# Layernorm of the next block moved between the gate and up steps of a gated MLP, with program order kept on three engines

## The chip, the cores and the metric

One core of one Trainium2 chip. The metric is the device time of one execution in microseconds, on the slowest (here the only) core. Profiled spans run from the first to the last instruction and are about 2 us shorter than the times.

## The reference, cut to what matters

```
xn = layernorm(x)                                  # x: 2048 x 640, bf16
s  = attention(xn)                                 # 32 heads of 192, last 512 keys, then @ wo
g  = silu((sigmoid(xn @ w_gate) * (xn @ w_up)) @ w_down)   # 640 -> 1536 -> 640
out = x + s * g
```

The kernel does the layernorm and the MLP first, in four blocks of 512 rows (g goes out to memory, the transposed xn stays on chip), then attention. The change touches the first part only.

## The kernel before: the parts concerned

One tile is 128 rows; a block has four. `xnT` is the transposed, normalised x that both parts read.

```python
def emit_ln_tile(i, xt, lnsb, lnps):
    xn = lnsb.tile([P, D], BF16, tag="xn")
    if i % 3 != 2:
        ...                                        # bn_stats x2, bn_aggr on DVE
    else:
        nc.scalar.activation(out=junk[:], in_=xt, func=ACT.Identity, accum_out=s12[:, 0:1])
        nc.scalar.activation(out=junk[:], in_=xt, func=ACT.Square, accum_out=s12[:, 1:2])
        ...                                        # three small DVE operations
    nc.scalar.activation(out=std[:], in_=var_ap, func=ACT.Sqrt, bias=eps_t[:], scale=1.0)
    nc.vector.reciprocal(out=rstd[:], in_=std[:])
    nc.vector.tensor_scalar(out=xn[:], in0=xt, ...)          # (x - mean) * rstd
    tps = lnps.tile([P, ND, P], BF16, tag="tps")             # one PSUM buffer
    for kt in range(ND):
        nc.tensor.transpose(tps[:, kt, :], xn[:, kt * P:(kt + 1) * P], ident[:])
    if i % 2 == 0:
        nc.scalar.copy(out=xnT[:, :, i * P:(i + 1) * P], in_=tps[:])
    else:
        nc.vector.tensor_copy(out=xnT[:, :, i * P:(i + 1) * P], in_=tps[:])
...
load_x(0)                                          # two buffers for x
...                                                # w_gate, w_up, w_down, one DMA each
load_x(1)
for tcn in range(NTC):                             # four blocks
    for tt in range(TPC):
        emit_ln_tile(tcn * TPC + tt, xt_c[:, tt, :], lnsb, lnps)
    if tcn + 2 < NTC:
        load_x(tcn + 2)
    for ft in range(NF):                           # twelve steps
        ...                                        # gps: 5 matmuls, ups: 5 matmuls
        nc.scalar.activation(out=sig[:], in_=gps[:], func=ACT.Sigmoid)
        nc.vector.tensor_tensor(out=hT[:, ft, :], in0=ups[:], in1=sig[:], op=ALU.mult)
    for tt in range(TPC):
        ...                                        # yps: w_down matmuls, silu, store g
```

The order on each engine is not that of the text: a scheduler sorts the instructions at compile time (in the trace of this kernel statistics of block 2 stand on ACT ahead of block 0's first copy, which starts at 26.02).

The softmax here doesn't subtract the row's maximum and nothing guards it: scores larger than these inputs give would overflow.

## Time and profile before

Median 1077.68 us of 4 runs. The prediction below shows the lines; this table puts the points in time together. "First" and "last" are starts of the first and ends of the last matmul, from the trace's order in time.

| us | before |
|---|---|
| first gate matmul of block 0 | 30.90 |
| 12 gate and up steps, blocks 0 to 3 | 27.83, 28.55, 27.75, 27.43 |
| gap from last w_down matmul to next first gate matmul | 4.57, 4.32, 4.32 |
| end of the MLP (last w_down matmul) | 207.6 |
| attention, from there to the end | 867.9 |

The step times run to the end of the last matmul; in a stream without gaps the next one starts about 0.16 us before that. In the gaps and the first 31 us PE has only the transposes to do. Attention is PE-bound (97% busy) and not touched.

### The profile page before, as it was taken

How to read it: one execution, taken by the hardware profiler on the slowest of the kernel's cores; microseconds unless marked ns; L12 is line 12 of the kernel's file. 1: busy time of each engine (PE TensorE's matmuls, PEld its weight loads, DVE VectorE, ACT ScalarE, POOL GpSimd, SP SyncE). 2: the span in 40 equal slices, each digit the busy share in tenths (PEclk: the TensorE clock that was granted, in tenths of full speed). 3: DMA queues.
4: the chain of work that ended last, by engine and by line, in shares of the span. 5: the costliest groups of instructions: out<-in, count | busy, mean ns of one | idle time of the engine just before them, and what ended most of it. 6: DMA issues, size and time to landing. Idle time of an engine off the chain costs nothing.

```text
span 1075.5 us, 18642 instructions
## 1 busy us (share of the span) xinstructions
PE 1014.6 (94%) x7362; PEld 579.6 (54%) x7472; DVE 426.8 (40%) x1545; ACT 439.7 (41%) x840; POOL 207.4 (19%) x337
## 2 busy tenths in 40 slices
PE   0989898999999999999999999999999999999998
PEld 0444444456565655555555555655555555555654
DVE  3433332245555520445445105445441055445502
ACT  3732222354545430265565203565561045565400
POOL 3000000233333210222222003222220032222000
PEclk9989999999999999999999999999999999999999
DMA  9200000284444334633233247233323563233042
GB/s 337 77 25 1 25 13 12 70 269 119 116 122 113 97 95 150 208 97 95 85 86 100 83 147 232 75 99 100 85 82 101 162 206 97 81 89 100 16 129 68
DMA packets 52039, 114.59 MB, mean 107 GB/s; under 512 B 5104, under 2 KB 34800, under 8 KB 51952
## 3 DMA queue, kind: packets, MB, share of 16 engines
q0 software_dynamic: 21424, 75.38, 23.9%
q1 hardware_dynamic: 30528, 38.01, 11.1%
q8 instruction: 58, 0.95, 0.4%
q14 instruction: 29, 0.24, 0.1%
HBM read 108.13 MB, written 5.24 MB: 105 GB/s over the span
## 4 chain that ended last, share of the span: by engine, by line
PE 77%; ACT 13%; issue 4%; DMA 4%; DVE 1%; POOL 0%; ACTq 0%; POOLq 0%
PE qps L254 20%; PE s_ps L326 19%; PE ops L291 16%; ACT pT L280 6%; ACT pT L279 5%; PE gps L174 5%; PE yps L193 5%; PE ups L179 5%; PE scB L273 2%; PE scA L270 2%; DMA xt<-in_A_x_dram 2%; PE scA L276 2%; DMA v_sb<-in_A_v_cache_dram 2%; PE kps L248 1%; ACT xnT L136 0%
## 5 line engine op out<-in xcount | busy, mean ns | idle before, releaser
L279 ACT ACTIVATE pT<-scA 128x512 bf16<-128x512 f32 x256 | 159.5, 623 | 209.4 <-PE scB L277 209.4
L254 PE MATMUL qps<-xnT,wq_sb 128*128 128x512 bf16 x901 | 214.3, 379 | 10.5 <-ACT pT L279 7.3
L326 PE MATMUL s_ps<-wo_sb,oT 128*128 128x128 bf16 (+1 forms) x1504 | 208.3, 297 | 2.5 <-ACT pT L279 0.5
L258 ACT CAST qT<-qps 128x512 bf16<-128x512 f32 x192 | 114.1, 594 | 231.7 <-PE qps L254 231.7
L297 DVE TENSOR_SCALAR o_sb<-ops,rden 128x192 bf16<-128x192 f32 x512 | 192.3, 407 | 4.5
L291 PE MATMUL ops<-v_sb,pT 128*128 128x193 bf16 x2048 | 181.5, 247 | 0.5 <-ACT pT L279 0.4
L291 PEld LDWEIGHTS <-pT 128*128 128x128 bf16 x2048 | 172.4, 98 | 15.9 <-ACT pT L279 1.0
L326 PEld LDWEIGHTS <-oT 128*128 128x128 bf16 x1536 | 118.1, 98 | 91.3 <-issue 2.0
L296 DVE RECIPROCAL rden<-ops 128x1 f32<-128x1 f32 x512 | 83.2, 163 | 204.2 <-PE ops L291 198.5
L280 ACT ACTIVATE pT<-scB 128x512 bf16<-128x512 f32 x256 | 161.7, 632 | 0.0
L254 PEld LDWEIGHTS <-wq_sb 128*128 128x128 bf16 x960 | 92.7, 97 | 111.5 <-issue 12.8
L310 DVE COPY oT<-otp 128x384 bf16<-128x384 bf16 x256 | 73.8, 349 | 102.6 <-PE otp L309 102.6
L228 POOL DMA_DIRECT2D wq_sb<-in_A_wq_dram x64 | 54.7, 854 | 278.3 <-PE qps L254 253.3
L233 POOL DMA_DIRECT2D v_sb<-in_A_v_cache_dram x128 | 96.3, 756 | 33.9 <-issue 23.8
L338 DVE TENSOR_TENSOR sg<-s_ps,gt 128x512 f32<-128x512 f32 (+1 forms) x32 | 14.2, 485 | 186.3 <-PE s_ps L326 183.1
L276 PE MATMUL scA<-qT,kTc 64*128 64x512 bf16 x256 | 77.1, 381 | 0.0
L277 PE MATMUL scB<-qT,kTc 64*128 64x512 bf16 x256 | 77.1, 381 | 0.0
L270 PE MATMUL scA<-qT,kTc 128*128 128x512 bf16 x255 | 76.6, 382 | 0.0
L273 PE MATMUL scB<-qT,kTc 128*128 128x512 bf16 x256 | 76.2, 379 | 0.1
L174 PE MATMUL gps<-xnT,wg_sb 128*128 128x512 bf16 x234 | 63.7, 400 | 3.2 <-DVE xnT L138 2.3
L185 DVE TENSOR_TENSOR hT<-ups,sig 128x512 bf16<-128x512 f32 x48 | 33.0, 691 | 77.7 <-PE ups L179 70.4
L179 PE MATMUL ups<-xnT,wu_sb 128*128 128x512 bf16 x235 | 61.3, 390 | 0.2
(54 smaller groups left out, 555.4 us busy)
## 6 DMA issues: line engine op xcount, KB each, us to landing
wq_sb<-in_A_wq_dram POOLq DMA_DIRECT2D x64, 480.0 KB, 4.2
wo_sb<-in_A_wo_dram SPq DMA_DIRECT2D x24, 1280.0 KB, 6.4
v_sb<-in_A_v_cache_dram POOLq DMA_DIRECT2D x128, 192.0 KB, 3.2
k_sb<-in_A_k_cache_dram POOLq DMA_DIRECT2D x32, 192.0 KB, 3.3
xt<-in_A_x_dram SPq DMA_DIRECT2D x4, 640.0 KB, 5.4
xt<-in_A_x_dram POOLq DMA_DIRECT2D x16, 160.0 KB, 3.5
gt<-g_dr POOLq DMA_DIRECT2D x16, 160.0 KB, 3.2
out_dram<-ot SPq DMA_DIRECT2D x16, 160.0 KB, 3.1
```

Of the source, the lines that this page charges most:

```text
L174: nc.tensor.matmul(gps[:], lhsT=wg_sb[:, kt, ft * P:(ft + 1) * P], rhs=xnT[:, kt, t0:t0 + TC], start=(kt == 0), stop=(kt == ND - 1),)
L179: nc.tensor.matmul(ups[:], lhsT=wu_sb[:, kt, ft * P:(ft + 1) * P], rhs=xnT[:, kt, t0:t0 + TC], start=(kt == 0), stop=(kt == ND - 1),)
L254: nc.tensor.matmul(qps[:, 0:TC], lhsT=wq_sb[:, kt, jj * P:(jj + 1) * P], rhs=xnT[:, kt, t0:t0 + TC], start=(kt == 0), stop=(kt == ND - 1),)
L258: nc.scalar.copy(out=qT[:, jj, :], in_=qps[:, 0:TC])
L270: nc.tensor.matmul(scA[st][:, 0:TC], lhsT=kTc[:, pr, 0, ss], rhs=qT[:, 0, :], start=True, stop=False)
L273: nc.tensor.matmul(scB[st][:, 0:TC], lhsT=kTc[:, pr, 2, ss], rhs=qT[:, 2, :], start=True, stop=False)
L276: nc.tensor.matmul(scA[st][:, 0:TC], lhsT=kTc[0:64, pr, 1, ss], rhs=qT[0:64, 1, :], start=False, stop=True)
L279: nc.scalar.activation(out=pTs[0][:, st, :], in_=scA[st][:, 0:TC], func=ACT.Exp, scale=SCALE)
L280: nc.scalar.activation(out=pTs[1][:, st, :], in_=scB[st][:, 0:TC], func=ACT.Exp, scale=SCALE)
L291: nc.tensor.matmul(ops[:, 0:DH + 1], lhsT=pT[:, st, ti * P:(ti + 1) * P], rhs=v_sb[:, st, hx, 0:DH + 1], start=(st == 0), stop=(st == NS - 1),
L297: nc.vector.tensor_scalar(out=o_sb[:, ti, hx * DH:(hx + 1) * DH], in0=ops[:, 0:DH], scalar1=rden[:, 0:1], scalar2=None, op0=ALU.mult,)
L326: nc.tensor.matmul(s_tiles[ti][ci][:, 0:cw], lhsT=oT[:, jt, ti * P:(ti + 1) * P], rhs=wo_sb[:, jl, cc0:cc0 + cw], start=(jt == 0), stop=(j ...
```

## The change

Its intent is to keep PE busy through the MLP: block 0's layernorm by a hand-written order, every later block's layernorm spread over the steps of the block ahead of it, and a fixed order so that the scheduler cannot undo it. With it come four x buffers in place of two, the gate and up weights in thirds, a dummy Sqrt at the beginning, and statistics of all later tiles on DVE.

```diff
-        tc.tile_pool(name="ln_x", bufs=2) as lnx,
+        tc.tile_pool(name="ln_x", bufs=4) as lnx,
+        tc.manual_schedule(engines={ENG.PE, ENG.Activation, ENG.DVE}),
...
-        nc.gpsimd.dma_start(out=wg_sb[:], in_=B_w_gate.rearrange("(kt p) f -> p kt f", p=P))
-        nc.gpsimd.dma_start(out=wu_sb[:], in_=B_w_up.rearrange("(kt p) f -> p kt f", p=P))
+        FCH = 3
+        for fc in range(FCH):
+            fs = slice(fc * F // FCH, (fc + 1) * F // FCH)
+            nc.gpsimd.dma_start(out=wg_sb[:, :, fs], in_=wg_v[:, :, fs])
+            nc.gpsimd.dma_start(out=wu_sb[:, :, fs], in_=wu_v[:, :, fs])
...
+        warm = lnsb.tile([P, 1], F32, tag="warm")
+        ln_std(warm[:], eps_t[:])                 # the dummy Sqrt
...                                                # block 0's layernorm, in a fixed order
+                if xt_n is not None:              # after step ft: the next block
+                    if ft < TPC:
+                        ...
+                        ln_stats(mv_n[:, ft, :], xt_n[:, ft, :], lnsb)
+                        if ft == TPC - 1:
+                            ln_std(std_n[:], mv_n[:, :, 1])
+                            nc.vector.reciprocal(out=rstd_n[:], in_=std_n[:])
+                    elif ft % 2 == 0:
+                        if ft > 4:
+                            tt = (ft - 6) // 2
+                            ln_tr((tcn + 1) * TPC + tt, xn_n, lnps, tt % 2 == 0)
+                        tt = (ft - 4) // 2
+                        xn_n = ln_norm(xt_n[:, tt, :], mv_n[:, tt, 0:1], rstd_n[:, tt:tt + 1], lnsb)
+                    elif ft == NF - 1:
+                        ln_tr((tcn + 1) * TPC + TPC - 1, xn_n, lnps, False)
```

`ln_stats`, `ln_std`, `ln_norm` and `ln_tr` are the parts of the old `emit_ln_tile`; `ln_tr` is the five transposes and the copy.

More of the change, by code (lines that the diff above doesn't have):

```diff
@@ L97 @@
     fsz = D // nchunk
-    def emit_ln_tile(i, xt, lnsb, lnps):
-        xn = lnsb.tile([P, D], BF16, tag="xn")
-        if i % 3 != 2:
-            stats = lnsb.tile([P, nchunk, nc.vector.BN_STATS_DIM], F32, tag="stats")
-            for c in range(nchunk):
-                nc.vector.bn_stats(out=stats[:, c, :], in_=xt[:, c * fsz:(c + 1) * fsz])
-            mv = lnsb.tile([P, nc.vector.BN_AGGR_DIM], F32, tag="mv")
-            nc.vector.bn_aggr(out=mv[:], in_=stats[:])
-            mean_ap = mv[:, 0:1]
-            var_ap = mv[:, 1:2]
-        else:
-            junk = lnsb.tile([P, D], BF16, tag="junk")
-            s12 = lnsb.tile([P, 2], F32, tag="s12")
-            nc.scalar.activation(out=junk[:], in_=xt, func=ACT.Identity, accum_out=s12[:, 0:1])
-            nc.scalar.activation(out=junk[:], in_=xt, func=ACT.Square, accum_out=s12[:, 1:2])
-            mvs = lnsb.tile([P, 2], F32, tag="mvs")
-            nc.vector.tensor_scalar(out=mvs[:, 0:1], in0=s12[:, 0:1], scalar1=1.0 / D, scalar2=None, op0=ALU.mult)
-            m2 = lnsb.tile([P, 1], F32, tag="m2")
-            nc.vector.tensor_tensor(out=m2[:], in0=mvs[:, 0:1], in1=mvs[:, 0:1], op=ALU.mult)
-            nc.vector.scalar_tensor_tensor(
-                out=mvs[:, 1:2], in0=s12[:, 1:2], scalar=1.0 / D, in1=m2[:],
-                op0=ALU.mult, op1=ALU.subtract,
-            )
-            mean_ap = mvs[:, 0:1]
-            var_ap = mvs[:, 1:2]
-        std = lnsb.tile([P, 1], F32, tag="std")
-        nc.scalar.activation(out=std[:], in_=var_ap, func=ACT.Sqrt, bias=eps_t[:], scale=1.0)
-        rstd = lnsb.tile([P, 1], F32, tag="rstd")
-        nc.vector.reciprocal(out=rstd[:], in_=std[:])
@@ new lines, in ln_stats, with ln_std, ln_norm @@
+    def ln_stats(mv_ap, xt, lnsb):
+        stats = lnsb.tile([P, nchunk, nc.vector.BN_STATS_DIM], F32, tag="stats")
+        for c in range(nchunk):
+            nc.vector.bn_stats(out=stats[:, c, :], in_=xt[:, c * fsz:(c + 1) * fsz])
+        nc.vector.bn_aggr(out=mv_ap, in_=stats[:])
+    def ln_std(std_ap, var_ap):
+        nc.scalar.activation(out=std_ap, in_=var_ap, func=ACT.Sqrt, bias=eps_t[:], scale=1.0)
+    def ln_norm(xt, mean_ap, rstd_ap, lnsb):
+        xn = lnsb.tile([P, D], BF16, tag="xn")
@@ L128, in emit_ln_tile, with ln_tr @@
         nc.vector.tensor_scalar(
-            out=xn[:], in0=xt, scalar1=mean_ap, scalar2=rstd[:],
-            op0=ALU.subtract, op1=ALU.mult,
-        )
+            out=xn[:], in0=xt, scalar1=mean_ap, scalar2=rstd_ap, op0=ALU.subtract, op1=ALU.mult,
+        )
+        return xn
+    def ln_tr(i, xn, lnps, on_act):
         tps = lnps.tile([P, ND, P], BF16, tag="tps")
@@ L134, in emit_ln_tile @@
             nc.tensor.transpose(tps[:, kt, :], xn[:, kt * P:(kt + 1) * P], ident[:])
-        if i % 2 == 0:
+        if on_act:
             nc.scalar.copy(out=xnT[:, :, i * P:(i + 1) * P], in_=tps[:])
@@ L138, in emit_ln_tile @@
             nc.vector.tensor_copy(out=xnT[:, :, i * P:(i + 1) * P], in_=tps[:])
+    ENG = mybir.EngineType
     with (
-        tc.tile_pool(name="ln_x", bufs=2) as lnx,
+        tc.tile_pool(name="ln_x", bufs=4) as lnx,
         tc.tile_pool(name="ln_sb", bufs=4) as lnsb,
@@ L147 @@
         tc.tile_pool(name="mlp_ps1", bufs=1, space=bass.MemoryType.PSUM) as mps1,
+        tc.manual_schedule(engines={ENG.PE, ENG.Activation, ENG.DVE}),
     ):
         xtiles = {}
-        def load_x(tcn):
+        for tcn in range(NTC):
             xt = lnx.tile([P, TPC, D], BF16, tag="xt")
@@ L154, in load_x @@
             xtiles[tcn] = xt
-        load_x(0)
-        nc.gpsimd.dma_start(out=wg_sb[:], in_=B_w_gate.rearrange("(kt p) f -> p kt f", p=P))
-        nc.gpsimd.dma_start(out=wu_sb[:], in_=B_w_up.rearrange("(kt p) f -> p kt f", p=P))
-        nc.gpsimd.dma_start(out=wd_sb[:], in_=B_w_down.rearrange("(kt p) d -> p kt d", p=P))
-        if NTC > 1:
-            load_x(1)
+        wg_v = B_w_gate.rearrange("(kt p) f -> p kt f", p=P)
+        wu_v = B_w_up.rearrange("(kt p) f -> p kt f", p=P)
+        FCH = 3
@@ new lines @@
+        for fc in range(FCH):
+            fs = slice(fc * F // FCH, (fc + 1) * F // FCH)
+            nc.gpsimd.dma_start(out=wg_sb[:, :, fs], in_=wg_v[:, :, fs])
+            nc.gpsimd.dma_start(out=wu_sb[:, :, fs], in_=wu_v[:, :, fs])
+        nc.gpsimd.dma_start(out=wd_sb[:], in_=B_w_down.rearrange("(kt p) d -> p kt d", p=P))
+        warm = lnsb.tile([P, 1], F32, tag="warm")
+        ln_std(warm[:], eps_t[:])
+        x0 = xtiles[0]
+        mv0 = [lnsb.tile([P, 2], F32, tag="mv", name=f"mv{t}") for t in range(4)]
@@ new lines, with norm0 @@
+        std0 = [lnsb.tile([P, 1], F32, tag="std", name=f"std{t}") for t in range(4)]
+        rstd0 = [lnsb.tile([P, 1], F32, tag="rstd", name=f"rstd{t}") for t in range(4)]
+        junk = lnsb.tile([P, D], BF16, tag="junk")
+        s12 = lnsb.tile([P, 2], F32, tag="s12")
+        m2 = lnsb.tile([P, 1], F32, tag="m2")
+        def norm0(t):
+            nc.vector.reciprocal(out=rstd0[t][:], in_=std0[t][:])
+            return ln_norm(x0[:, t, :], mv0[t][:, 0:1], rstd0[t][:], lnsb)
+        nc.scalar.activation(out=junk[:], in_=x0[:, 2, :], func=ACT.Identity, accum_out=s12[:, 0:1])
@@ new lines @@
+        ln_stats(mv0[0][:], x0[:, 0, :], lnsb)
+        ln_std(std0[0][:], mv0[0][:, 1:2])
+        nc.scalar.activation(out=junk[:], in_=x0[:, 2, :], func=ACT.Square, accum_out=s12[:, 1:2])
+        ln_stats(mv0[1][:], x0[:, 1, :], lnsb)
+        ln_std(std0[1][:], mv0[1][:, 1:2])
+        n0 = norm0(0)
+        n1 = norm0(1)
+        ln_tr(0, n0, lnps, True)
+        nc.vector.tensor_scalar(out=mv0[2][:, 0:1], in0=s12[:, 0:1], scalar1=1.0 / D, scalar2=None, op0=ALU.mult)
+        nc.vector.tensor_tensor(out=m2[:], in0=mv0[2][:, 0:1], in1=mv0[2][:, 0:1], op=ALU.mult)
@@ L162 @@
+        nc.vector.scalar_tensor_tensor(
+            out=mv0[2][:, 1:2], in0=s12[:, 1:2], scalar=1.0 / D, in1=m2[:], op0=ALU.mult, op1=ALU.subtract,
+        )
+        ln_stats(mv0[3][:], x0[:, 3, :], lnsb)
+        ln_std(std0[2][:], mv0[2][:, 1:2])
+        ln_std(std0[3][:], mv0[3][:, 1:2])
+        ln_tr(1, n1, lnps, True)
+        n2 = norm0(2)
+        ln_tr(2, n2, lnps, True)
+        n3 = norm0(3)
+        ln_tr(3, n3, lnps, False)
         for tcn in range(NTC):
             t0 = tcn * TC
-            xt_c = xtiles.pop(tcn)
@@ L165 @@
-            for tt in range(TPC):
-                emit_ln_tile(tcn * TPC + tt, xt_c[:, tt, :], lnsb, lnps)
-            if tcn + 2 < NTC:
-                load_x(tcn + 2)
+            xt_n = xtiles.get(tcn + 1)
+            xn_n = None
             hT = mh.tile([P, NF, TC], BF16, tag="hT")
@@ L185 @@
                 nc.vector.tensor_tensor(out=hT[:, ft, :], in0=ups[:], in1=sig[:], op=ALU.mult)
+                if xt_n is not None:
+                    if ft < TPC:
+                        if ft == 0:
+                            mv_n = lnsb.tile([P, TPC, 2], F32, tag="mvn")
+                            std_n = lnsb.tile([P, TPC], F32, tag="stdn")
+                            rstd_n = lnsb.tile([P, TPC], F32, tag="rstdn")
+                        ln_stats(mv_n[:, ft, :], xt_n[:, ft, :], lnsb)
[10 more added lines that the diff above has]
+                        ln_tr((tcn + 1) * TPC + TPC - 1, xn_n, lnps, False)
             for tt in range(TPC):
```

## The prediction

Its sum is: 16.9 + 13.2 + 6.0 - 3.4 - 0.5 = 32.2 us, and 1077.7 - 32.2 = 1045.5.

> **What bounds the kernel now.** I read the page first: which engine is full, and where it is not.
>
> ```profile
> PE 1014.6 (94%) x7362; PEld 579.6 (54%) x7472; DVE 426.8 (40%) x1545; ACT 439.7 (41%) x840; POOL 207.4 (19%) x337
> PE   0989898999999999999999999999999999999998
> ```
>
> PE is nearly full, so time can be won only where it is not: the first slice (27 us) and slices 3, 5 and 7, all in the first 208 us, the MLP stage that the diff edits. Next, the busy time by stretch, cut at the first matmul of each of the four 512-row blocks and at the last one before it (columns: PE, PEld, DVE, ACT, POOL busy, granted clock, DMA share, GB/s).
>
> ```profile
> 0.00:30.90 30.90, 2.79 (x20) 2.14 (x21) 12.86 (x57) 13.14 (x33) 11.43 (x21) 1.00 0.96 330
> 71.40:76.10 4.70, 2.00 (x23) 1.48 (x21) 3.52 (x12) 3.06 (x5) 0.55 (x1) 0.82 0.09 35
> 117.50:122.00 4.50, 1.81 (x24) 1.33 (x22) 3.04 (x8) 1.84 (x4) 0.54 (x1) 1.00 0.10 36
> 162.70:167.10 4.40, 1.72 (x23) 1.24 (x21) 1.87 (x4) 1.75 (x4) 0.54 (x1) 0.94 0.10 37
> 207.70:1075.50 867.80, 844.69 (x6436) 495.41 (x6527) 357.74 (x1378) 366.58 (x706) 192.17 (x309) 1.00 0.39 116
> ```
>
> So there are four holes: 31 us before block 0 and about 4.5 us before each of the other three. Attention (last row) takes 868 us at full clock with PE at 97%; the diff has no line there. The chain of waits says what fills the first hole:
>
> ```profile
> 0.74 4.42 DMA xt<-in_A_x_dram
> 5.19 1.28 DVE stats L104 x3
> ...
> 11.89 13.38 DMA xt<-in_A_x_dram
> 25.29 0.83 ACT junk L112 x2
> 26.12 0.58 ACT xnT L136
> ```
>
> The x of block 0 lands at 5.16, but 13.4 us go to another load of x, begun at 11.89. That is the third block's (two buffers, so it waits for block 0's x to be used up). Block 0 does not need it. The order on ACT makes it wait: the waits of PE give the price.
>
> ```profile
> PE tps L134 <- ACT xnT L136: 23.0, 8, 17.4
> PE tps L134 <- DVE xn L128: 8.6, 1, 8.6
> PE gps L174 <- DVE xnT L138: 2.3, 4, 0.6
> ```
>
> The longest wait, 17.4 us, is for an ACT copy of transposed x. The timeline shows tile 0 transposed at 8.62 to 9.34 and copied only at 26.02: ACT was given statistics of block 2 ahead of it, and stood still until that x came. The remaining 5.6 us of the row are copies between transposes, one PSUM buffer for all, at the three later boundaries and in block 0.
>
> [...] the ready copy sat 16.7 us behind a waiting instruction. [...] at 30.90, 76.12, 122.03 and 167.14 the first matmuls start 0.43 us apart, then 0.216, and the clock records say 0.5 for 6.8, 3.4 and 3.4 us around the three later boundaries. [...] The trace has 11 loads in this stage, 1283 ns each[...] (37.75 to 40.65 us holds two loads and the Sqrts: 2.9 us). [...] while block 2's x and w_down ran together (16 to 23 us), they shared, x getting 20% of the time; but at the start x of blocks 0 and 1 (1.3 MB) ran alone to 5.6 us, though w_gate was issued at 1.29.
>
> **The change, part by part.**
>
> *Start.* PE, ACT and DVE now keep program order, so block 2's statistics cannot overtake block 0's copies. I lay the new chain out with durations of the old trace. x lands at 5.16 as before (first in its queue). A dummy Sqrt loads the table during the load of x; so the 1.28 us load at 6.03 is out of the way (Identity and Square ran after the Sqrt load without another). Tile 0: two bn_stats (0.43 start to start) and aggregate (0.2) to 6.4; Sqrt 0.29, to 6.75, while DVE does tile 1's statistics to 7.45; reciprocal 0.15 and normalise 0.44, to 8.05. First transpose about 8.1 (before: 8.62). Then the single PSUM buffer sets the pace: cold transposes 0.70, copy 0.67 on ACT or 0.49 on DVE, two semaphores of 0.04 to 0.1, so 1.47 per tile on ACT, 1.27 on DVE (measured 28.02 minus 26.75). Tile 1 starts at 9.6; its copy stands in ACT's order behind tile 3's Sqrt, whose statistics DVE ends at about 10.2; so it ends at 11.2. Tiles 2 and 3: 11.3 and 12.75; first gate matmul 12.75 + 1.27 = **14.0**. Gain 30.9 - 14.0 = **16.9 us**.
>
> Are the weights there? They now come in thirds, 0.655 MB each. With four x buffers all four loads of x queue at once, so blocks 2 and 3 compete with them. If these share as at 16 to 23 us (0.29 MB/us for weights, from 5.8): gate third at about 8.6, up third at 10.9. If x runs first as at the start: its 2.62 MB at 0.37 MB/us end near 9.7, gate third 12, up third 14, needed at 16. Either way before PE, and each next third has 4 x 2.16 = 8.6 us of matmuls before it. This needs waits by region of a tile, which the trace shows: at 149.83 w_down matmuls read hT while its last slice was still being written (149.89 to 150.58).
>
> *Boundaries.* Statistics, normalising and transposes of the next block move between the 12 steps of this block's gate and up matmuls. Removed: gaps from last yps to first gps, 71.55 to 76.12, 117.71 to 122.03, 162.82 to 167.14: 4.57 + 4.32 + 4.32 = **13.2 us**. With the gap goes the half clock. A warm step is 2.158 us (11 steps from 170.83 to 194.57), so 12 are 25.9; blocks 1 to 3 took 28.55, 27.75 and 27.43 from first gps to first yps: 2.65 + 1.85 + 1.53 = **6.0 us**. Added on PE: 12 sets of five transposes in the stream at 0.055 each (12 kps transposes fill 0.66 us), 12 x 0.28 = **3.4 us**.
>
> *Room on the others.* Per step of 2.16 us DVE has hT 0.69, and in steps 0 to 3 two bn_stats and an aggregate, 1.1: 1.8 in all, it fits. ACT has 0.60 and sometimes a 0.69 copy. The tight place is step 3: Sqrt waits for all statistics, 1.9 us after the up matmuls of step 3, then Sqrt 0.29 and a Sigmoid load 1.28 (the Sqrt load fits in the wait). Sigmoid 4 then ends 4.15 us after that point and frees the bank for gate step 6, which starts at 4.3. Just hidden; I allow 0.17 us in each of three blocks, **0.5 us**.
>
> Sum: 16.9 + 13.2 + 6.0 - 3.4 - 0.5 = **32.2 us**. Cross-check: 14.0 + 4 x (25.9 + 13.04) + 1.8 cold at the start + 3.4 + 0.5 = 175.5 for the end of the MLP against 207.6. Time: 1077.7 - 32.2 = **1045.5 us**.
>
> **Rivals.** (a) Weights take over the wait: if a matmul waits for whole weight tiles, or small pieces run slower, PE starts near 20, when both (3.93 MB at 0.29 from 5.8) are in; about 1051. For: DMA share is 0.96 in the first 31 us. Against: the region waits above, and pieces of 5 x 1024 bytes per partition are near w_down's 5120-byte packets, which kept 354 GB/s (my working: 16 engines, 231 ns each). (b) Fixed order stalls PE inside the blocks: the table switch, or a transpose waiting for its input. One lost step per block, 3 x 2.2, makes 1052. For: margins of 0.2 us at step 3. Against: block 0 of before had two table loads and four passes over x on ACT from 36.16 to 40.65, and PE lost only 0.17 us. (c) The MLP gains but attention gives some back: another order of its instructions, or its prefetches (now behind three times as many weight loads on POOL) late. For: POOL already waits 4.1 us for w_gate to land before a ninth load. Against: there are over 150 us until the first is used. Worth perhaps plus or minus 4 us. (d) Only the start gains and the boundaries stay serial: 1061; it would need the copies or normalisations to slip past the block, against 2.16 us steps with over half of ACT free.
>
> **Range and chances.** The start is good to 1.5 us, the clock recovery to 1 us, stalls inside blocks 0 to 5 us, attention 2 us: low 1040, high 1052. The 2% line is 1056.1; it would take (a) and (b) together or (d). Chances: faster 0.93, same 0.06, slower 0.01.
>
> **What would show it.** First gate matmul at 14 (19 or later: rival a, with a DMA of w_gate or w_up ahead of PE). First yps about 27.7 us later, then blocks repeating every 40 us instead of 45 to 46, with no half clock after about 18. No PE wait for an xnT copy after block 0. Waits of gps or ups for sig or hT around the fifth to seventh steps would be (b). MLP end at 175.5 and attention 868 long; a different length there is (c). I am wrong on mechanism if blocks still take 45 us.

## The result, and the profile after

1045.34 us (median of 8, 1044.31 to 1045.78) against 1077.77 (12 runs): a ratio of 0.9701, 95% interval 0.9691 to 0.9711. Ratios in this document are the mean time of one kernel's fast runs over that of the other's in the same rounds, so not quite the ratio of the medians quoted. Predicted: 1045.5.

The page's PE rows, busy share and busy tenths by slice:

```profile
PE 1007.9 (97%) x7362; PEld 578.2 (55%) x7472; DVE 430.4 (41%) x1535; ACT 429.0 (41%) x814; POOL 211.7 (20%) x341
PE   5999999999999999999999999999999999999998
```

The zero of the first slice is a 5 and the 8s are gone. PE's busy time fell by only 6.7 us while the span fell by 32: most of the gain is idle time, the rest matmuls no longer at half clock.

Busy time by stretch, cut at the first gate matmul of each block (columns as in the prediction):

```profile
0.00:14.20 14.20, 2.79 (x20) 2.14 (x21) 6.83 (x22) 7.43 (x14) 9.62 (x17) 1.00 0.89 298
56.40:96.50 40.10, 39.84 (x235) 20.29 (x238) 18.15 (x39) 14.85 (x26) 1.10 (x2) 1.00 0.05 17
...
175.60:1043.50 867.90, 844.70 (x6437) 495.62 (x6527) 358.20 (x1378) 366.75 (x706) 190.59 (x305) 1.00 0.39 116
```

A block now takes 40.0 us in place of 45 to 46 and PE is busy in all of it, with DVE at 18 us of 40. Attention takes 867.9 us, to the tenth what it took.

The chain of waits over the start:

```profile
0.74 4.37 DMA xt<-in_A_x_dram
...
10.83 0.59 ACT xnT L120
...
11.46 0.70 PE tps L118 x5
12.19 0.70 ACT xnT L120
...
12.94 0.71 PE tps L118 x5
13.67 0.50 DVE xnT L122
...
14.21 2.29 PE gps L194 x5
```

No DMA stands in it but the first x. From 5.1 to 10.5 us (left out above) nearly every piece is DVE, with statistics and normalises; from 10.8 us on it is the pattern of one PSUM buffer: copy, transpose, copy, transpose. And the waits of PE in the MLP:

```profile
PE tps L118 <- DVE rstd L160: 8.2, 1, 8.2
PE tps L118 <- ACT xnT L120: 2.6, 3, 1.1
PE gps L194 <- DVE xnT L122: 0.6, 1, 0.6
```

All five waits are in block 0's layernorm (one of 8.2, three summing to 2.6, one of 0.6). In blocks 1 to 3 PE waits for nothing. The first line names DVE's reciprocal; what PE really waited for is the normalise after it, which ends at 8.16 (the first transpose starts at 8.22).

### The profile page after: what moved, and what is told of

Same layout as the page of the kernel before. It is cut to its first block, busy times and chain, and to the rows that moved or that the text cites. A ratio compares the mean times of both kernels' runs of the same rounds, so it can differ in the third digit from the quotient of the medians.

```text
span 1043.5 us, 18610 instructions
## 1 busy us (share of the span) xinstructions
PE 1007.9 (97%) x7362; PEld 578.2 (55%) x7472; DVE 430.4 (41%) x1535; ACT 429.0 (41%) x814; POOL 211.7 (20%) x341
## 4 chain that ended last, share of the span: by engine, by line
PE 79%; ACT 12%; issue 4%; DMA 3%; DVE 1%; POOL 1%; ACTq 0%; POOLq 0%; DVEq 0%
PE qps L292 20%; PE s_ps L364 19%; PE ops L329 16%; ACT pT L318 6%; ACT pT L317 5%; PE ups L199 5%; PE yps L231 5%; PE gps L194 5%; DMA v_sb<-in_A_v_cache_dram 3%; PE scB L311 2%; PE scA L308 2%; PE scA L314 2%; PE kps L286 1%; DMA xt<-in_A_x_dram 1%; PE tps L118 0%
## 5 line engine op out<-in xcount | busy, mean ns | idle before, releaser
L292 PE MATMUL qps<-xnT,wq_sb 128*128 128x512 bf16 x901 | 214.3, 379 | 10.5 <-ACT pT L317 7.3
L376 DVE TENSOR_TENSOR sg<-s_ps,gt 128x512 f32<-128x512 f32 (+1 forms) x32 | 14.2, 485 | 186.2 <-PE s_ps L364 183.0
L347 PEld LDWEIGHTS <-o_sb 128*128 128x128 bf16 x768 | 45.7, 97 | 27.7 <-issue 26.7
L194 PE MATMUL gps<-xnT,wg_sb 128*128 128x512 bf16 x230 | 59.9, 385 | 1.1 <-DVE xnT L122 0.6
```

What stands on the lines that cost most here:

```text
L194: nc.tensor.matmul(gps[:], lhsT=wg_sb[:, kt, ft * P:(ft + 1) * P], rhs=xnT[:, kt, t0:t0 + TC], start=(kt == 0), stop=(kt == ND - 1),)
L292: nc.tensor.matmul(qps[:, 0:TC], lhsT=wq_sb[:, kt, jj * P:(jj + 1) * P], rhs=xnT[:, kt, t0:t0 + TC], start=(kt == 0), stop=(kt == ND - 1),)
```

## The experiments

All outputs are right. Times are medians beside runs of the kernel before on the same chip (1077.5 to 1077.7 each time).

### 1. The kernel before with four x buffers

```diff
-        tc.tile_pool(name="ln_x", bufs=2) as lnx,
+        tc.tile_pool(name="ln_x", bufs=4) as lnx,
```

> The kernel before with four buffers for x in place of two, nothing else. Theory (the order of instructions on ACT and DVE makes block 0 wait, not the late load of block 2's x): the scheduler, free to, places statistics of still later blocks ahead of block 0's copies, and the x of block 3 lands only near 25 us, so the first gate matmul stays at 27 us or later and the time within 4 us of before: about 1075. Rival (the 13.4 us load of block 2's x, late for want of a buffer, is the cause): the first gate matmul comes near 15 to 18 us and the time falls by 12 us or more, to 1065 or less.

Measured: 1077.36 us, ratio 1.000 (0.9985 to 1.0015). The first gate matmul started at 31.5. ACT in order of time:

```profile
20.84 0.28 ACT L125 ACTIVATE std<-mv,eps_t 128x1 f32<-128x1 f32 x1
25.18 0.74 ACT L112 ACTIVATE junk<-xt 128x640 bf16<-128x640 bf16 x1 [4.06 <-DMA xt<-in_A_x_dram]
...
26.78 0.67 ACT L136 COPY xnT<-tps 128x640 bf16<-128x640 bf16 x1
```

With four x buffers the scheduler put statistics of the last block too ahead of block 0's first copy, and ACT waited for that x until 25.18. The want of a buffer was not the cause; these lines show that the order on ACT was. The lesson in reading: the chain showed a late load, and a late load was indeed the longest piece, yet loading earlier bought nothing.

### 2. The kernel before in program order

```diff
+        tc.manual_schedule(engines={mybir.EngineType.PE, mybir.EngineType.Activation, mybir.EngineType.DVE}),
```

> The kernel before with its program order kept on PE, ACT and DVE, nothing else. Theory: the start gains (first gate matmul about 16 us in place of 30.9) but each later block's whole layernorm becomes serial at its boundary: gaps of about 12 us in place of 4.4, 3 x 7.7 = 23 us lost. Sum: about 1086. Rival (keeping program order is what gains in the change): 1062 or less.

Measured: 1090.93 us, ratio 1.0126 (1.0109 to 1.0143): slower. The first gate matmul came at 16.14, as expected; the boundaries were worse than expected:

```profile
56.30:70.60 14.30, 2.88 (x21) 1.91 (x21) 7.79 (x24) 6.86 (x13) 0.56 (x1) 0.61 0.05 14
110.90:126.40 15.50, 2.87 (x21) 1.92 (x22) 7.21 (x24) 8.40 (x17) 0.54 (x1) 0.60 0.03 11
167.80:179.30 11.50, 2.60 (x20) 1.74 (x21) 7.65 (x24) 6.74 (x13) 0.54 (x1) 0.68 0.04 16
```

11.5 to 15.5 us with PE busy under 3. So the old scheduler was right at the boundaries (it had statistics done early there) and wrong at the start. Keeping the old text's order costs more than it gains.

### 3. The changed kernel with the scheduler free

```diff
-        tc.manual_schedule(engines={ENG.PE, ENG.Activation, ENG.DVE}),
```

> The changed kernel with the scheduler free again (only the line that keeps program order taken out). Theory: the interleaved boundaries survive (its PE order still has the transposes between the steps), but statistics of blocks 1 to 3 go ahead of block 0's last copies and first hT on DVE and ACT; the first gate matmul comes near 19 us and the first steps wait for DVE: about 1052 (1049 to 1056). Rival (moving the text is enough): 1045, like the changed kernel.

Measured: 1048.11 us (1047.56 to 1049.34), ratio 0.9727 (0.9713 to 0.9742); 2.8 us over the changed kernel, less than half of what I had expected. The blocks still take 40 us. Only the start slipped, to 16.28, and DVE shows why (chain of waits of this run):

```profile
13.74 0.11 DVE mv_n L103
...
14.21 0.18 DVE rstd_n L214
...
14.69 1.15 DVE xn L110 x3
15.83 0.41 DVE xnT L122
16.28 2.29 PE gps L193 x5
```

Block 1's statistics (`mv_n`), the first of block 2's and three of block 1's normalisations went ahead of block 0's last copy, at 15.83. I had expected those of block 3 there too, and first steps that wait for DVE; neither came. So the new text carries nearly all of the gain, and the fixed order the last 2.8 us. What in the new text tamed the scheduler at the start was not separated: the statistics of later tiles that no longer sit on ACT, the x loaded at once, or the finer split of the layernorm.

### 4. The transposes put back to the boundary

```diff
-                        if ft > 4:
-                            tt = (ft - 6) // 2
-                            ln_tr((tcn + 1) * TPC + tt, xn_n, lnps, tt % 2 == 0)
...                                                # after the block's w_down matmuls:
+            if xt_n is not None:
+                for tt in range(TPC):
+                    ln_tr((tcn + 1) * TPC + tt, xns[tt], lnps, tt % 2 == 0)
```

> The changed kernel with the transposes and copies of the next block put back to the boundary; statistics and normalising stay between the steps, and so does the new start. Theory: three gaps of about 4.4 us, half clock after each for about 2 us, less 1.1 us of transposes that leave the stream: 3 x 5.3 = 16 us, about 1061; the start as in the changed kernel (14.2 us), so before minus this, about 16.5 us, is the start's share. Rival (statistics and normalising were what held the boundaries): under 1050.

Measured: 1060.99 us, ratio 0.9845 (0.9831 to 0.986). The first gate matmul is at 14.19, so this kernel has the new start and the old boundaries. It splits the gain: 1077.5 - 1061.0 = 16.5 us for the start, 1061.0 - 1045.3 = 15.7 us for the boundaries (predicted 16.9 and 15.3). PE in order of time at the first boundary:

```profile
54.99 0.44 PE L118 MATMUL tps<-ident,xn 128*128 128x128 bf16 x5
56.22 0.44 PE L118 MATMUL tps<-ident,xn 128*128 128x128 bf16 x5 [0.78 <-ACT xnT L120]
57.24 0.44 PE L118 MATMUL tps<-ident,xn 128*128 128x128 bf16 x5 [0.58 <-DVE xnT L122]
58.46 0.44 PE L118 MATMUL tps<-ident,xn 128*128 128x128 bf16 x5 [0.78 <-ACT xnT L120]
59.48 0.59 PE L194 MATMUL gps<-xnT,wg_sb 128*128 128x512 bf16 x1 [0.58 <-DVE xnT L122]
```

Nothing is late here but the hand-over through one PSUM buffer, and PE's next matmuls run at half clock (the clock records have 0.5 from 59.0 to 62.4 us, and for 3.4 and 6.8 us at the next two boundaries). The 12 steps after the three gaps take 27.3, 27.0 and 28.5 us in place of 25.9. The gaps (4.3, 4.6 and 4.6 us) are as long as those of the kernel before, so there too statistics and normalising were not what the boundary waited for.

### 5. Two of the four transposes at the boundary

The same edit, for tiles 2 and 3 of each block only.

> As the run with all four transposes at the boundary, but only two of the four tiles there. Theory [...]: gaps of about 2.3 us, no half clock, 3 x (2.3 - 0.56) = 5.2 us over the changed kernel, about 1050.6. Rival (the loss goes with the number of transposes at the boundary, clock included): half of the 15.7 us of the run with four, about 1053.2; with the half clock after each gap it would be 1056.

Measured: 1050.72 us, ratio 0.9756 (0.9739 to 0.9774), as the sum had it. The three boundaries, about 2.1 us each from the last w_down matmul to the first gate matmul:

```profile
56.30:58.60 2.30, 0.94 (x15) 0.70 (x13) 1.38 (x3) 1.13 (x3) 0.55 (x1) 1.00 0.00 0
98.00:100.40 2.40, 1.04 (x16) 0.79 (x14) 1.38 (x3) 1.17 (x3) 0.54 (x1) 1.00 0.00 0
139.80:142.10 2.30, 0.94 (x15) 0.70 (x13) 1.38 (x3) 1.11 (x3) 0.60 (x2) 1.00 0.04 7
```

The granted clock stays 1.00 and the next matmuls run 0.216 us apart at once. Half the transposes cost a third (5.4 of 15.7 us): the second half brings the half clock with it.

### 6. Gate and up weights in one piece each

```diff
-        FCH = 3
+        FCH = 1
```

> The changed kernel with w_gate and w_up each loaded in one piece again. Theory (the prediction's: weights compete with x of blocks 2 and 3; w_gate whole lands near 12.6 us, w_up near 19): the first gate matmuls stay at 14.2, the first up matmuls wait from 16.5 to about 19.3, and half clock lasts some longer: 2.8 to 4.8 us slower than the changed kernel, about 1049. Rival (weights are hidden in any case, the thirds are worth nothing): 1045.3.

Measured: 1050.25 us, ratio 0.975 (0.9733 to 0.9768): 4.9 us over the changed kernel, 0.1 over the range. The waits of PE have a new line:

```profile
PE ups L199 <- DMA wu_sb<-in_B_w_up_dram: 3.5, 1, 3.5
```

w_up came at 19.5 us for a first use at 16.1, and PE stayed at half clock until 25.3 where the changed kernel is at full clock from 18.6. Without the thirds, rival (a) of the prediction would have been near the truth, at about the price it named (1051).

### 7. A second table switch at step 3

```diff
                             ln_std(std_n[:], mv_n[:, :, 1])
+                            sw = lnsb.tile([P, 2], F32, tag="sw")
+                            nc.scalar.activation(out=sw[:, 0:1], in_=eps_t[:], func=ACT.Sigmoid)
+                            ln_std(sw[:, 1:2], eps_t[:])
```

> The changed kernel with one more Sigmoid and Sqrt of a 128x1 tile after the Sqrt of step 3 of blocks 0 to 2: two more table loads of 1.28 us and two activations of 0.29 us, about 3.1 us of ACT, per block. Theory (the table switch in the change is only just hidden, 0.1 us before gate step 6 needs its bank): PE stalls 3.0 us in each of three blocks, about 9 us slower than the changed kernel, 1054. Rival (ACT is busy 41% and has room to hide it): 1045.5.

Measured: 1059.32 us (1057.27 to 1060.71), ratio 0.9831 (0.9806 to 0.9856): 14.0 us over the changed kernel, more than either side. ACT of the changed kernel at that place, then PE's longest wait in this run:

```profile
24.72 1.28 ACT L106 ACT_TABLE_LOAD   x1
27.01 0.30 ACT L106 ACTIVATE std_n<-mv_n,eps_t 128x4 f32<-128x4 f32 x1 [1.01 <-DVE mv_n L103]
27.33 1.28 ACT L204 ACT_TABLE_LOAD   x1
28.62 1.08 ACT L204 ACTIVATE sig<-gps 128x512 bf16<-128x512 f32 x2
```

```profile
PE gps L194 <- ACT sig L204: 8.8, 3, 2.9
```

In the changed kernel the first of the two Sigmoids ends near 29.2 and PE starts the gate matmuls that need its bank at 29.30: hidden by 0.1 us, as worked out. 3.1 us more of ACT turned into 2.9 us of PE in each of three blocks, though ACT is busy 41% of the span: its mean share says nothing about this place. The other 5 us is half clock, for 3.4 us after each stall by the trace's clock records (at 33.0, 77.4 and 121.8 us). I had not expected a 2.9 us wait to bring it.

The length of a wait is not all that counts. In all 14 traces the edges of the clock records lie on a grid of 3.41 us (in the kernel before, the records from 33.41 on last 40.96, 6.83, 40.96, 3.41, 40.96 and 3.41 us). Up to the end of the MLP, once the clock was full, it fell after each of the 15 grid stretches in which PE was busy 10 to 51% of the time (51, 42 and 38% in the kernel before), and after none with 60% or more. The waits of this run left 14, 20 and 30%; the gaps of run 5 left 60% or more, also where one lay wholly inside a stretch (98.08 to 101.49 us). So in none of the stretches before a fall was PE idle throughout.

### 8. Four PSUM banks for block 0's transposes

```diff
-        ln_tr(0, n0, lnps, True)
+        ln_tr(0, n0, mps, True, "gps")
...
         ln_std(std0[2][:], mv0[2][:, 1:2])
-        ln_std(std0[3][:], mv0[3][:, 1:2])
-        ln_tr(1, n1, lnps, True)
+        ln_tr(1, n1, mps, True, "gps")
+        ln_std(std0[3][:], mv0[3][:, 1:2])
         n2 = norm0(2)
-        ln_tr(2, n2, lnps, True)
+        ln_tr(2, n2, mps, True, "ups")
```

> The changed kernel with block 0's four transposes in four PSUM banks (those of the gate and up tiles, idle then) and tile 1's copy ahead of tile 3's Sqrt on ACT. Theory (after the change the start is paced by one PSUM buffer: transpose, copy, transpose): the last transposes follow DVE's last normalise at 11.7 us and the first gate matmul comes near 13.1 in place of 14.2: 1.1 us faster than the changed kernel, 1044.2. Rival (DVE's chain of statistics and normalising sets the start): no change, 1045.3.

Measured: 1044.2 us, ratio 0.9692 (0.9674 to 0.971); the interval overlaps the changed kernel's. The edit does two things, the banks and tile 1's copy ahead of tile 3's Sqrt on ACT; what each is worth was not separated.

### 9. The changed kernel, the four banks again, and a PE kept busy, side by side

The third kernel adds, on top of the four banks, 71 matmuls on a constant whose sums nobody reads: 46 before block 0's first transpose, the rest between the transposes and before the first gate matmul.

```diff
+        def keep_busy(n):
+            for _ in range(n):
+                nc.tensor.matmul(idle[:, 0:256], lhsT=ones[:, 0:P], rhs=ones[:], start=True, stop=True)
+        keep_busy(46)
```

> The changed kernel itself, beside the next three on the same chip: 1045.3 under every theory.

> The kernel with four PSUM banks at the start, now beside the changed kernel on the same chip: 1.1 us under it (theory: one PSUM buffer paces the start), or the same within 0.3 us (rival: noise between calls).

> Four banks at the start, and PE kept busy from 1 us on with matmuls of a constant whose results nobody reads (about 70 of 256 columns, also between block 0's transposes). Theory (the first steps' half clock, 2.3 us, comes from PE being idle before them): the first gate matmul near 12.7 and at full clock; 2.6 us under the four-banks kernel, 1041.6. Rival (the idle stretches between block 0's transposes bring the half clock back, or the extra matmuls hold up the transposes): 1044 or more.

Measured, in this order: 1045.28 us (ratio 0.9701, 0.9688 to 0.9715), 1043.82 (0.9687, 0.9673 to 0.97) and 1042.32 (0.9673, 0.966 to 0.9686). With four banks the first gate matmul is at 12.99 (changed kernel: 14.19), and all five times lie under all four of the changed kernel's; the intervals still overlap. The trace shows a start 1.2 us earlier, but the two profiles end the MLP at 174.74 and 175.00: the half clock at the start lasted to 18.03 with four banks and to 17.35 without. The changed kernel's own two profiles differ by 0.6 us there (175.62 and 175.00), so 1.1 to 1.5 us is a rough size. The kernel with the busy PE is clear of the changed kernel, 3.0 us faster. PE in order of time:

```profile
1.22 7.91 PE L158 MATMUL idle<-ones 128*128 128x256 bf16 x46 [1.22 <-DVE ones L153]
8.97 0.44 PE L118 MATMUL tps<-ident,xn 128*128 128x128 bf16 x5
...
13.22 1.24 PE L207 MATMUL gps<-xnT,wg_sb 128*128 128x512 bf16 x5 [0.24 <-DVE xnT L122]
14.29 1.24 PE L212 MATMUL ups<-xnT,wu_sb 128*128 128x512 bf16 x5
```

The first five gate matmuls fill 1.08 us in place of 2.1: full clock from the first. The 46 were too many: they end at 9.13, and the first transpose, possible at 8.2, waits till 8.97. The expected 1041.6 was missed by about that.

### 10. Without the dummy Sqrt

```diff
-        warm = lnsb.tile([P, 1], F32, tag="warm")
-        ln_std(warm[:], eps_t[:])
```

> The changed kernel without the dummy Sqrt ahead of the first x. Theory: ACT loads another table first and Sqrt's 1.28 us load comes after Identity, at 5.9; the first Sqrt ends near 7.5 in place of 6.6, DVE's first reciprocal waits 0.4 and its second 0.2 more, and the start slips 0.5 to 0.7 us: about 1045.9. Rivals: the whole 1.28 us shows (1046.6), or nothing does (1045.3).

Measured: 1045.87 us (1044.41 to 1046.03), ratio 0.97 (0.9686 to 0.9713), the same as with it. My theory fell; "nothing shows" was right. DVE in order of time, first in the changed kernel, then in this one:

```profile
7.32 0.85 DVE L110 TENSOR_SCALAR xn<-xt,mv,rstd 128x640 bf16<-128x640 bf16 x1
8.26 0.76 DVE L110 TENSOR_SCALAR xn<-xt,mv,rstd 128x640 bf16<-128x640 bf16 x1
```

```profile
7.49 0.16 DVE L158 RECIPROCAL rstd<-std 128x1 f32<-128x1 f32 x1 [0.34 <-ACT std L106]
7.69 0.45 DVE L110 TENSOR_SCALAR xn<-xt,mv,rstd 128x640 bf16<-128x640 bf16 x1
8.39 0.16 DVE L158 RECIPROCAL rstd<-std 128x1 f32<-128x1 f32 x1 [0.26 <-ACT std L106]
8.60 0.45 DVE L110 TENSOR_SCALAR xn<-xt,mv,rstd 128x640 bf16<-128x640 bf16 x1
```

Without the dummy, DVE does wait for the late table (0.34 and 0.26 us), and starts the first normalise 0.37 us later. But it ends at 8.14, against 8.17 with it, and the first gate matmul is at 14.24, against 14.21. The same normalise takes 0.85 us when it starts at 7.32 (0.95 and 0.97 in two other runs, from 7.19 and 7.18) and 0.45 when it starts at 7.69: always done by 8.14 to 8.17. In the changed kernel POOL was issuing the w_down load from 6.97 to 8.02.

The same is seen in the other kept traces: up to 215 us, all 27 normalises of the 14 traces that took more than 0.5 us ended 0.12 to 0.15 us after the end of a POOL instruction that issues a DMA. In run 6, where such instructions end earlier, at 7.68 and 8.43, the first two normalises end at 7.84 and 8.58 (changed kernel: 8.16 and 9.02, after 8.01 and 8.87), and its first gate matmul is at 13.77. Why a normalise takes longer there, no run shows. What run 10 shows is that the time saved on ACT was not passed on by DVE.

## Why the prediction was right, by its own steps

- **Where the time sits.** Right. Four holes before; after, only the one at the start, of 14.2 us; attention 867.9 us in both.
- **The start, 30.9 to 14.0.** Measured 14.21: 16.7 us in place of 16.9. The pacing by one PSUM buffer is what the chain shows from 10.8 us on, and run 8 fits it: with four banks, and one Sqrt moved, 12.99. Up to 10.5 us DVE sets the pace, and the agreement there is in part luck: DVE reached the first normalise 0.3 us sooner than laid out (7.32, not about 7.6), and it took 0.85 us in place of 0.44. Two parts of the story were off. Keeping program order is not by itself the reason (run 3: the new text without it loses 2.8 us, run 2: it without the new text loses 13.4 us); and the dummy Sqrt bought nothing (run 10). That late x was a symptom of order, not the cause, holds: run 1.
- **Weights.** "Either way before PE": right, with room. POOL's wait for the first gate third ended at 10.3 us (predicted 8.6 if x and weights share, 12 if x goes first; needed at 14.2), each further third about 2.5 us later. Counted from the trace's packets, x of blocks 0 and 1 ran alone to 6 us, then the queues shared: 0.09 MB/us for x, 0.265 for the weights, in packets of 4096 bytes, not 5120. Run 6 shows that the thirds were needed.
- **The boundaries, 13.2 + 6.0 - 3.4 - 0.5.** The gaps went to zero. The steps of blocks 1 and 2 take 27.0 us with transposes (25.9 + 4 x 0.28), those of block 3, which carries none, 25.9: all of the half clock came back, and the transposes cost what was worked out. (Of the 6.0 us, 3 x 0.16 belong to the gaps, since the step times ended with the last matmul; the sum is the same.) Runs 4 and 5 show the two terms apart.
- **Stalls inside blocks, 0.5.** Measured 0. The tight place is where it was put, with 0.1 us to spare; run 7 shows what lies behind it. One reading for rival (b) was off: in the stretch that it cites ACT made two passes over x (from 36.05 to 37.73), not four.
- **Half clock at the start, 1.8.** Measured, from the first gate matmul to the first w_down matmul, 2.1 in the profile shown (29.15 - 25.9 - 1.12) and 1.5 in that of the same kernel in run 9 (28.56 - 25.9 - 1.12): the first gate matmul is at 14.2 in both, but full clock came at 18.57 and at 17.35. So the term was sized within the scatter between executions.
- **Sum.** End of the MLP 175.6, predicted 175.5; the repeat has 175.0. The mechanism holds term by term; a sum right to 0.1 us is luck.

## What to carry to other kernels

Before you load earlier or add buffers for a wait on a DMA, ask which instruction stands in line in front of the one that PE needs: the transfer at the end of the chain may belong to work that nobody needs yet. Work between stages for which the other engines have room (here it brought DVE to 18 us and ACT to 15 us of a 40 us block) can be hidden by writing it between the steps of the stage ahead; what then remains is the gap you leave. Here gaps of 2.9 us and more cost their length plus 1.1 to 2.6 us of half clock (runs 4 and 7), while gaps of 2.1 us with transposes in them cost only their length (run 5); no length between was tried. A low mean share of an engine (ACT's 41% here, run 7) is no slack: look at the one place where its queue must be through by a given time.

## What else the traces show

- Half clock. It came after 3.41 us stretches with PE busy 10 to 51%, and followed a wait of 2.9 us, which left 14 to 30%, three times out of three (run 7); it followed a boundary of 2.1 us with two sets of transposes in it, which left 60% or more, none out of three (run 5).
- Table loads. Every ACT_TABLE_LOAD took 1283 ns, 12 in the kernel before and 9 in the changed kernel. In the changed kernel the load at 27.33 ends at 28.61 and the Sigmoid starts at 28.62.
- First packets. With no other transfer under way, the first packet of seven stores of g from POOL in the kernel before ran 1.11 to 1.14 us after the issue. But the first weight load was issued at 1.29 us and its first packet ran at 5.6, when the x queue, issued at 0.74, was nearly empty (894 of the 1024 packets of blocks 0 and 1 begun); and block 2's x, issued by SyncE at 11.89 while the weights were coming, had its first packet at 15.5. So with another queue full the first packet came about 4 us after the issue, both times; why, no run here tells.
- Normalises beside a DMA issue on POOL. Not every one is longer: in run 1 a normalise ran from 7.76 to 8.18, at its usual 0.43 us, inside an issue that ran from 7.67 to 8.48, and the next one, from 8.10, ended at 8.61. In run 8 one ran from 10.55 to 11.00, in 0.45 us, inside an issue from 10.47 to 11.29.
